# Bucket projections in four column parts, weight conversions in three stages, the queries' low part on GpSimd

## The chip, the cores and the metric

The kernel runs on one core of one Trainium2 chip. The metric is the device time of that core in microseconds (us). An engine name stands for its queue too: PE is TensorE, DVE is VectorE, ACT is ScalarE, POOL is GpSimd and SP is SyncE, which here only issues DMAs. Each engine works its own list of instructions strictly in order, and an instruction whose operands aren't there holds up everything behind it on its engine.

## The reference, cut to what matters

Two batches, 8 heads, 768 rows, head dimension 64, six hash bits. Attention is masked by bucket: a query sees a key only if the signs of their six projections agree. Two feed-forward blocks follow.

```python
q_bits = (np.einsum('bhsd,dk->bhsk', q, proj) > 0)      # six bits each
k_bits = (np.einsum('bhsd,dk->bhsk', k, proj) > 0)
mask = q_bucket[:, :, :, None] == k_bucket[:, :, None, :]
scores = np.where(mask, scale * q @ k.T, -1e9)
attn = softmax(scores); out = attn @ v
x = moe(out)      # relu(x w_in) = u, v; LayerNorm(v); w_spatial v + b; u * v; w_out
y = x + relu(LayerNorm(x) * g @ w_ch1) @ w_ch2
```

## The kernel before, in words

Everything is in single precision made of two parts: a value is rounded to a high part in TensorE's fp32r format, and what is left over is the low part; products are made as high*high + high*low + low*high. The weights arrive as 64-bit floats and are turned into single precision on the chip.

**Attention** is 96 tiles of 128 queries: batch, head, group of two tiles (order, line 249). A pair of heads (b, r), heads 2r and 2r+1, is loaded together, transposed, as 128 rows (two heads of 64) by 768 columns. Of a pair, pair_load (206) fetches k and q into the slot where later the low part stands; mismatch (236) multiplies the raw data by a small matrix of signs, `side`, and turns the result by one comparison into rows of 0, 1 or 2**60 (tile `m`); pair_split (218) makes the high parts on POOL (line 228, first pair: ACT), the keys' low part on POOL in two halves (86) and the queries' low part on DVE (234). The low part overwrites the raw data, so it waits for mismatch's matmuls. passes_of (258) lets SP copy high, low and mismatch rows into the operand tiles ks (a head's keys) and qs (a group's queries), lines 269, 270 and 275. A tile then goes through scores (L299, PE), masked_max (L310, DVE), exps (L323, ACT), transposes (L337 PE, L340 ACT, L342 DVE) and weighted (L351 PE, L356 ACT, L358 DVE).

The steps of a pair come a fixed number of tiles ahead of its first tile: AT = (-10, -7, -6, -4, 0) for load, mismatch, split, first and second head's ks. qs of a group is made QA + 1 = 4 tiles ahead.

**Conversions.** Twelve pieces of the weights w_out, w_in's v half and w_in's u half are converted during the attention (conversions, line 484; names out, v, u). Each is a DMA by ACT's queue (stage), one ACT and five DVE instructions (words_f64, lines 102 to 107), a sum on POOL (111), then a high part on ACT (80) and a low part on POOL (86). CONV_AT gives the tile at which a piece's words are issued, CONV_D the four steps' distances from it, (-1, 0, 3, 3). There is one buffer (CB0 = 1) for a piece.

**Feed-forward.** From tile M0 = 60 on, moe1 of batch 0 is interleaved (pv, pg, py on PE); after the attention come moe1 of batch 1 and the last block with w1 and w2 (pc and acc), whose pieces are converted as they come (load_f64).

The order of each engine's list is not that of the source: a scheduler runs through a model of the engines and lists instructions as they become ready there; issue_after keeps some of them behind the last max or exp.

Of the kernel before, what the change touches and what calls it, by code (L numbers as in the profile page):

```python
# [8 lines left out]
F32 = mybir.dt.float32  # L9
# [8 lines left out]
P = 128  # L18
# [11 lines left out]
def attn_moe_kernel(ctx: ExitStack, tc: tile.TileContext, qT, kT, v, proj, w_in, w_spT, b_sp, w_out, g_ln, w1, w2, out):  # L30
# [18 lines left out]
    CONV_D = (-1, 0, 3, 3)  # L49
# [46 lines left out]
    def words_f64(st, nm):  # L96

        a, n = st.shape[1], st.shape[2]
# [19 lines left out]
    def load_f64(dst_hi, dst_lo, src, nm):  # L118

        split_f64(dst_hi, dst_lo, join_f64(*words_f64(stage_f64(src, nm), nm)))  # L120
# [14 lines left out]
    K_FROM, Q_FROM = 38, 0  # L135
    M_AT = {"k": (D, NB), "q": (D + 32, 32 + NB)}
    sides = const.tile([P, K_FROM + P], F32, name="sides")
    nc.gpsimd.memset(sides, 0.0)
    for own, at in zip((slice(0, D), slice(D, P)), M_AT["q"]):
        for i, sign in enumerate((1.0, -1.0, 1.0)):  # L140
            nc.gpsimd.tensor_scalar(
                sides[own, at + i * NB : at + (i + 1) * NB], pj[own], sign, 0.0, op0=ALU.mult, op1=ALU.add
            )
    side = {"k": sides[:, K_FROM : K_FROM + P], "q": sides[:, Q_FROM : Q_FROM + P]}
# [3 lines left out]
    for t, fills in (  # L148
        (above, ((0, P, 0.0), (0, NM, -TINY), (32, NB + NM, -TINY), (32, NM, 0.0), (D, NB, -TINY))),
        (above, ((D + 32, NM, -TINY), (D + 32, NB, 0.0))),  # L150
        (worth, ((0, P, 1.0), (32, NB + NM, MASKED), (D + 32, NM, MASKED))),
    ):
        for at, n, value in fills:
            nc.gpsimd.memset(t[at : at + n], value)
# [63 lines left out]
    def pair_split(b, r, first=False):  # L218

        for nm in "kq":  # L220
# [8 lines left out]
            if nm == "k" and not first:  # L229
# [6 lines left out]
    def mismatch(b, r):  # L236


        m = ap.tile([P, S], F32R, tag="m", name=f"m_{b}_{r}", bufs=2)
# [215 lines left out]
    def converted(src, dst, nm, after=None):  # L455
# [6 lines left out]
        def words():  # L462
            d["tc"] = words_f64(d["st"], nm)
# [411 lines left out]
```

## Time and profile before

| | us |
|---|---|
| median of 3 runs | 736.6 (736.15 to 738.83) |
| the profiled execution's own time | 737.13 |
| its span, first to last instruction | 734.9 |
| PE, DVE, ACT, POOL busy | 686.0, 438.7, 303.6, 190.9 |
| mean granted clock of TensorE | 0.98 of 2.4 GHz |

The table gives one core's engines over the whole span. A share of the span is a mean over stages: the attention lasts until about 347 us, where the last weighted sum (po) is seen, and the feed-forward alone fills what follows. PE is busy 93% of the span, so the shares say that PE's work, not its waiting, is most of the time; which of it can go is read from the stages.

### The profile page before, as it was taken

How to read it: one execution, taken by the hardware profiler on the slowest of the kernel's cores; microseconds unless marked ns; L12 is line 12 of the kernel's file. 1: busy time of each engine (PE TensorE's matmuls, PEld its weight loads, DVE VectorE, ACT ScalarE, POOL GpSimd, SP SyncE). 2: the span in 40 equal slices, each digit the busy share in tenths (PEclk: the TensorE clock that was granted, in tenths of full speed). 3: DMA queues.
4: the chain of work that ended last, by engine and by line, in shares of the span. 5: the costliest groups of instructions: out<-in, count | busy, mean ns of one | idle time of the engine just before them, and what ended most of it. 6: DMA issues, size and time to landing. Idle time of an engine off the chain costs nothing.

```text
span 734.9 us, 9990 instructions
## 1 busy us (share of the span) xinstructions
PE 686.0 (93%) x3580; PEld 533.1 (73%) x3580; DVE 438.7 (60%) x849; ACT 303.6 (41%) x583; POOL 190.9 (26%) x182
## 2 busy tenths in 40 slices
PE   6999999898999999998889999799988999999997
PEld 5767667675767777776678887587766788888885
DVE  3698987897665645444798459676899712112112
ACT  2676766685556545344364222453323201100100
POOL 2234143334352222110144243244544400000000
PEclk8899999999999999999999999899999999999999
DMA  6765866674554554212625153523232101001001
GB/s 168 187 159 155 248 163 179 207 195 122 156 175 98 178 179 102 80 38 72 220 62 197 44 165 122 199 90 114 89 112 86 58 1 57 1 0 58 1 0 58
DMA packets 51922, 84.37 MB, mean 115 GB/s; under 512 B 6970, under 2 KB 36206, under 8 KB 50850
## 3 DMA queue, kind: packets, MB, share of 16 engines
q1 hardware_dynamic: 38834, 54.37, 25.8%
q10 hardware_dynamic: 13040, 29.36, 12.3%
q8 instruction: 29, 0.48, 0.3%
q14 instruction: 19, 0.16, 0.1%
HBM read 51.12 MB, written 12.58 MB: 87 GB/s over the span
## 4 chain that ended last, share of the span: by engine, by line
PE 60%; DVE 15%; DMA 11%; ACT 4%; issue 4%; POOL 3%; SPq 1%; DVEq 0%; ACTq 0%; POOLq 0%
PE acc L747 12%; PE pc L437 11%; PE sc L299 7%; DMA f_w<-in_w 7%; PE pv L437 7%; PE pt L337 6%; PE pg L607 6%; PE po L351 6%; PE py L437 3%; POOL f64c_w L111 2%; DVE f_w L105 2%; DVE x L310 2%; DMA qs<-q 2%; DMA f_v<-in_w_in 1%; DVE f64c_w L107 1%
## 5 line engine op out<-in xcount | busy, mean ns | idle before, releaser
L747 PE MATMUL acc<-w2t,ch 128*128 128x512 f32 x576 | 145.3, 398 | 6.6 <-DVE ch L738 5.2
L437 PE MATMUL pc<-xh,w1t 128*128 128x512 f32 x576 | 146.9, 400 | 3.9 <-DVE xh L731 2.7
L747 PEld LDWEIGHTS acc<-w2t,ch 128*128 128x128 f32 x576 | 107.5, 189 | 34.5 <-DVE ch L738 8.1
L437 PEld LDWEIGHTS pc<-xh,w1t 128*128 128x128 f32 x576 | 110.0, 192 | 30.0 <-ACT f64c_w L102 2.9
L310 DVE TENSOR_SCALAR_CACHE_REDUCE x<-sc 128x768 f32<-128x768 f32 x96 | 89.5, 950 | 23.1 <-PE sc L299 22.9
L323 ACT ACTIVATE x<-x,nb 128x768 f32<-128x768 f32 x96 | 89.3, 931 | 32.7 <-DVE x L310 32.6
L738 DVE SCALAR_TENSOR_TENSOR ch<-pc,ch 128x512 fp32r<-128x512 f32 x48 | 33.0, 688 | 112.6 <-ACT ch L737 112.6
L299 PE MATMUL sc<-ks,qs 128*128 128x512 f32 (+3 forms) x384 | 86.3, 363 | 9.2 <-PE po L351 3.1
L337 PE MATMUL pt<-ident,x 128*128 128x128 f32 x576 | 79.8, 278 | 9.8 <-ACT x L323 9.3
L337 PEld LDWEIGHTS pt<-ident,x 128*128 128x128 f32 x576 | 67.6, 143 | 26.7 <-ACT x L323 17.6
L737 ACT ACTIVATE ch<-pc 128x512 fp32r<-128x512 f32 x48 | 28.5, 593 | 131.5 <-PE pc L437 131.5
L299 PEld LDWEIGHTS sc<-ks,qs 128*128 128x128 f32 (+1 forms) x384 | 59.8, 199 | 21.6 <-PE po L351 6.2
L351 PE MATMUL po<-e,vv 128*64 128x256 f32 x576 | 74.1, 393 | 0.4 <-DVE m L246 0.4
L111 POOL TENSOR_TENSOR f64c_w<-f_w,f64c_w 128x512 f32<-128x512 f32 x32 | 43.7, 1368 | 93.9 <-DVE f64c_w L107 77.9
L340 ACT ACTIVATE e<-pt 128x384 f32<-128x384 f32 x96 | 46.5, 488 | 45.4 <-PE pt L337 44.5
L342 DVE COPY e<-pt 128x384 f32<-128x384 f32 x96 | 52.7, 549 | 20.7 <-PE pt L337 20.2
L351 PEld LDWEIGHTS po<-e,vv 128*64 128x64 f32 x576 | 37.5, 138 | 24.4 <-issue 7.3
L102 ACT ACTIVATE f64c_w<-f_w 128x512 f32<-128x512 f32 x32 | 21.4, 669 | 63.0 <-DMA f_w<-in_w 59.6
L607 PE MATMUL pg<-vn,w_sp 128*128 128x512 f32 x180 | 44.1, 397 | 0.0
L437 PE MATMUL pv<-w_u,act_x 128*128 128x512 f32 x144 | 37.8, 398 | 4.7 <-DMA w_u<-ws_u 2.8
L607 PEld LDWEIGHTS pg<-vn,w_sp 128*128 128x128 f32 x180 | 33.3, 188 | 7.6
L437 PE MATMUL py<-w_out,act_g 128*128 128x512 f32 x144 | 35.8, 396 | 2.1 <-ACT act_g L426 2.1
(131 smaller groups left out, 813.3 us busy)
## 6 DMA issues: line engine op xcount, KB each, us to landing
f_w<-in_w ACTq DMA_DIRECT2D x32, 512.0 KB
ks<-k SPq DMA_DIRECT2D x48, 192.0 KB
qs<-q SPq DMA_DIRECT2D x144, 64.0 KB
wst_sp<-in_w_spT SPq DMA_DIRECT2D x12, 384.0 KB
w_out<-ws_out SPq DMA_DIRECT2D x2, 2048.0 KB
vv<-in_v SPq DMA_DIRECT2D x16, 192.0 KB
ot<-y_dram SPq DMA_DIRECT2D x12, 256.0 KB
out<-ot SPq DMA_DIRECT2D x12, 256.0 KB
```

Of the source, the lines that this page charges most:

```text
L111: nc.gpsimd.tensor_tensor(cf, tf, cf, op=ALU.add)
L299: nc.tensor.matmul(sc[:, csl], qs[:rows, i, qsl], ks[:rows, i, csl], start=(i == 0), stop=(i == 1))
L310: last["max"] = nc.vector.tensor_scalar(x, t["sc"], MASKED, FMAX, op0=ALU.min, op1=ALU.min, accum_out=nb,).ins
L323: last["exp"] = nc.scalar.activation(t["x"], t["x"], AF.Exp, bias=t["nb"], scale=-1.0, accum_out=z_sum[b][:, n, h : h + 1]).ins
L337: nc.tensor.transpose(pt[:, i, :], t["x"][:, kt * P : (kt + 1) * P], ident)
L340: nc.scalar.activation(e, pt, AF.Copy)
L342: nc.vector.tensor_copy(e, pt)
L351: nc.tensor.matmul(po[a : a + D, :GW], heads[b, h]["vv"][:, kt], gr["e"][:, kt], start=(kt < 2), stop=(kt >= NKT - 2))
L437: mm = nc.tensor.matmul(ps, lh(i), rh(j), start=(n == 0), stop=(n == tot - 1)).ins
L607: nc.tensor.matmul(pg, w[i][:, k], vn[:, j, k, :], start=(n == 0), stop=(n == len(order3) - 1))
L738: last["lo"] = nc.vector.scalar_tensor_tensor(ch[:, 1], pc, 0.0, ch[:, 0].bitcast(F32), op0=ALU.max, op1=ALU.subtract).ins
L747: last["mm"] = nc.tensor.matmul(accs[c][t], ch[:, i, t * P : (t + 1) * P], w2t[f][:, j, 0, :], start=(start and n == 0), stop=(stop and n ...
```

## The change: what it does

**1. Projections.** `side` is now 32 columns wide for keys and for queries (`sides` has 38 columns instead of 166), and the eight matmuls of a pair write four parts of 32 partitions each of one 128x512 PSUM tile: keys of one half, keys of the last third, queries of one half, queries of the last third, 256 columns at a time. Before, four matmuls with 128 weight columns over 384 data columns filled two 128x384 tiles, keys and queries accumulated. One comparison over 128x512 takes the place of two over 128x384. The mismatch rows of columns 512 to 767 lie in other partitions than those of columns 0 to 511, so ks takes two copies for them.

**2. qs.** The high part goes to both its places by one DMA with a repeated source: three DMAs a group instead of four; ks has five instead of four.

**3. Conversions.** words_f64 became a generator with three stages: ACT's instruction and the first DVE one; two DVE ones; the last two. CONV_D is (-1, 0, 1, 2, 4, 4): the stages are one tile apart, sum and finish one tile later than before.

**4. The queries' low part** of all pairs but the first is made by POOL: one more instruction scales the raw queries in place (128x768), and two subtract the high part (128x384 each). DVE's instruction of line 234 remains for the first pair alone.

```diff
-    CONV_D = (-1, 0, 3, 3)
+    CONV_D = (-1, 0, 1, 2, 4, 4)
...
         nc.vector.tensor_scalar(cf, cf, F64_MIN, F64_MAX, op0=ALU.max, op1=ALU.min)
+        yield
         nc.vector.tensor_scalar(c, c, 3, 0x3FFFFFFF, op0=ALU.logical_shift_left, op1=ALU.bitwise_and)
         nc.vector.scalar_tensor_tensor(hi, hi, 0xC0000000, c, op0=ALU.bitwise_and, op1=ALU.bitwise_or)
+        yield
         nc.vector.tensor_scalar(c, hi, 0xFF800000, None, op0=ALU.bitwise_and)
         nc.vector.scalar_tensor_tensor(cf, lo, 2.0**-52, cf, op0=ALU.mult, op1=ALU.mult)
-        return hi.bitcast(F32), cf
+        yield hi.bitcast(F32), cf
...
-    sides = const.tile([P, K_FROM + P], F32, name="sides")
+    sides = const.tile([P, NB + QUAD], F32, name="sides")
...
-            if nm == "k" and not first:
+            if not first:
+                if nm == "q":
+
+                    nc.gpsimd.tensor_scalar(raw, raw, scale, 0.0, op0=ALU.mult, op1=ALU.add)
                 for c in range(2):
                     csl = slice(c * KC, (c + 1) * KC)
                     split_lo(lo[:, csl], raw[:, csl], hi[:, csl])
...
-        for c in range(2):
-            csl = slice(c * KC, (c + 1) * KC)
-            pm = ps_b.tile([P, 512], F32, tag="b", name=f"pm_{b}_{r}_{c}")
-            for i, nm in enumerate("kq"):
+        m = ap.tile([P, 2 * GW], F32R, tag="m", name=f"m_{b}_{r}", bufs=2)
+        pm = ps_b.tile([P, 2 * GW], F32, tag="b", name=f"pm_{b}_{r}")
+
+        for half in range(2):
+            for n, (nm, g) in enumerate((("k", half), ("k", 2), ("q", half), ("q", 2))):
                 raw = pairs[b, r][nm, "raw"]
-                nc.tensor.matmul(pm[:, :KC], side[nm], raw[:, csl], start=(i == 0), stop=(i == 1))
-            nc.vector.tensor_scalar(m[:, csl], pm[:, :KC], above, worth, op0=ALU.is_gt, op1=ALU.mult)
+                out_n = pm[n * QUAD : (n + 1) * QUAD, half * GW : (half + 1) * GW]
+                nc.tensor.matmul(out_n, side[nm], raw[:, g * GW : (g + 1) * GW], start=True, stop=True)
+        nc.vector.tensor_scalar(m, pm, above, worth, op0=ALU.is_gt, op1=ALU.mult)
...
+            nc.sync.dma_start(out=t[0:D].bitcast(F32), in_=two[own, 0:1, sl].to_broadcast([D, 2, n]))
+            nc.sync.dma_start(out=t[D:P, 0].bitcast(F32), in_=two[own, 1, sl])
...
-        return stage, words, join, finish
+        return stage, words, words, words, join, finish
```

On PE, at the mismatch of pair (0, 1), the four matmuls of the kernel before stand between the weighted sum of a group (po) and the next transposes (pt); pm is the PSUM tile.

```order
L351 MATMUL po_0_1_350<-e_0_1_245,vv_0_175 64x256 x6
L245 MATMUL pm_1_0_361<-k_0_1_270,sides 128x384
L245 MATMUL pm_1_0_361<-q_0_1_272,sides 128x384
L245 MATMUL pm_1_1_365<-k_0_1_270,sides 128x384
L245 MATMUL pm_1_1_365<-q_0_1_272,sides 128x384
L337 MATMUL pt_1_0_0_0_377<-ident,x_1_0_0_346 128x128 x3
```

In the changed kernel the same place holds eight, in the order keys, keys, queries, queries, twice.

```order
L366 MATMUL po_0_1_356<-e_0_1_253,vv_0_184 64x256 x6
L252 MATMUL pm_1_367<-k_0_1_277,sides 32x256 x2
L252 MATMUL pm_1_367<-q_0_1_279,sides 32x256 x2
L252 MATMUL pm_1_367<-k_0_1_277,sides 32x256 x2
L252 MATMUL pm_1_367<-q_0_1_279,sides 32x256 x2
L352 MATMUL pt_1_0_0_0_381<-ident,x_1_0_0_352 128x128 x3
```

The place is the same; only the matmuls themselves and their shapes differ.

On DVE, at the same pair, a whole conversion (f_out and f64c_out), both comparisons (m), the queries' low part (q) and a sum (xT) stand in one run ahead of the max of the next tile (x_1_1_0) in the kernel before.

```order
L103 TENSOR_SCALAR f64c_out_369<-f64c_out_369 128x512
L104 TENSOR_SCALAR f64c_out_369<-f64c_out_369 128x512
L105 SCALAR_TENSOR_TENSOR f_out_330<-f_out_330,f64c_out_369 128x512
L246 TENSOR_SCALAR m_1_360<-pm_1_0_361,above,worth 128x384
L358 TENSOR_TENSOR xT_177<-po_0_1_350,ol_0_1_357 64x256
L106 TENSOR_SCALAR f64c_out_369<-f_out_330 128x512
L246 TENSOR_SCALAR m_1_360<-pm_1_1_365,above,worth 128x384
L234 SCALAR_TENSOR_TENSOR q_0_1_272<-q_0_1_272 128x768
L107 SCALAR_TENSOR_TENSOR f64c_out_369<-f_out_330,f64c_out_369 128x512
L310 TENSOR_SCALAR x_1_1_0_420,nb_1_1_0_421<-sc_1_1_0_387 128x768
```

In the changed kernel the max of that tile stands after four instructions of this work, and the conversion's last two come behind it, each after a max.

```order
L104 TENSOR_SCALAR f64c_out_377<-f64c_out_377 128x512
L106 TENSOR_SCALAR f64c_out_377<-f64c_out_377 128x512
L253 TENSOR_SCALAR m_1_366<-pm_1_367,above,worth 128x512
L107 SCALAR_TENSOR_TENSOR f_out_336<-f_out_336,f64c_out_377 128x512
L373 TENSOR_TENSOR xT_186<-po_0_1_356,ol_0_1_363 64x256
L357 COPY e_1_0_380<-pt_1_0_0_1_386 128x3x128
L325 TENSOR_SCALAR x_1_1_0_427,nb_1_1_0_428<-sc_1_1_0_391 128x768
L109 TENSOR_SCALAR f64c_out_377<-f_out_336 128x512
L325 TENSOR_SCALAR x_1_1_1_459,nb_1_1_1_460<-sc_1_1_0_391 128x768
L357 COPY e_1_0_380<-pt_1_0_1_1_418 128x3x128
L110 SCALAR_TENSOR_TENSOR f64c_out_377<-f_out_336,f64c_out_377 128x512
```

What moved is the max, from behind nine instructions to behind six.

On POOL, at pair (1, 1), where the first block of batch 0 also begins (act_x are its low parts, f64c_u and w_u a conversion's), the kernel before has the keys' low part (k_1_1) as its only low part.

```order
L86 TENSOR_TENSOR act_x_0_2192<-xT_177,act_x_0_2192 128x512
L86 TENSOR_TENSOR act_x_1_2195<-xT_177,act_x_1_2195 128x512
L228 TENSOR_SCALAR q_1_2_2296<-q_1_2_2296 128x768
L86 TENSOR_TENSOR act_x_2_2245<-xT_177,act_x_2_2245 128x512
L86 TENSOR_TENSOR k_1_1_1851<-k_1_1_1851 128x384 x2
L111 TENSOR_TENSOR f64c_u_1816<-f_u_1786,f64c_u_1816 128x512
```

In the changed kernel the queries' scaling follows the keys' low part, and four other instructions stand between it and the queries' low part (q_1_1).

```order
L86 TENSOR_TENSOR act_x_0_2195<-xT_186,act_x_0_2195 128x512
L86 TENSOR_TENSOR k_1_1_1854<-k_1_1_1854 128x384 x2
L235 TENSOR_SCALAR q_1_1_1856<-q_1_1_1856 128x768
L86 TENSOR_TENSOR act_x_1_2198<-xT_186,act_x_1_2198 128x512
L86 TENSOR_TENSOR act_x_2_2253<-xT_186,act_x_2_2253 128x512
L114 TENSOR_TENSOR f64c_u_1669<-f_u_1637,f64c_u_1669 128x512
L231 TENSOR_SCALAR q_1_2_2303<-q_1_2_2303 128x768
L86 TENSOR_TENSOR q_1_1_1856<-q_1_1_1856 128x384 x2
```

The keys' low part moved ahead of two of the act_x instructions; the queries' low part, before on DVE, comes last of the eight.

## Rows read from the trace of the kernel before

**Rows 1.** The page, part 1: busy us (share of the span) xinstructions.

```profile
PE 686.0 (93%) x3580; PEld 533.1 (73%) x3580; DVE 438.7 (60%) x849; ACT 303.6 (41%) x583; POOL 190.9 (26%) x182
```

**Rows 2.** Stretches: length, busy us of each engine, PEclk, DMA share, GB/s.

```profile
50.00:100.00 50.00, 47.15 (x323) 34.63 (x322) 44.95 (x96) 35.19 (x74) 18.65 (x18) 1.00 0.66 194
100.00:150.00 50.00, 45.29 (x306) 33.19 (x306) 41.90 (x93) 32.45 (x68) 15.01 (x15) 0.97 0.65 182
150.00:200.00 50.00, 46.25 (x299) 34.03 (x299) 39.06 (x85) 33.17 (x70) 20.20 (x18) 1.00 0.56 144
200.00:250.00 50.00, 48.76 (x290) 37.40 (x290) 28.38 (x70) 27.44 (x57) 16.40 (x16) 1.00 0.56 170
```

**Rows 3.** Chain that ended last, from 0 to 280 us: start us, us, what.

```profile
8.77 4.25 DMA qs<-q
...
37.47 1.21 DVE q L234
...
63.18 1.45 PE po L351 x12
64.62 2.78 PE pm L245 x8
...
158.26 3.38 DMA qs<-q
```

**Rows 4.** Timeline of PE, 33 to 42.5 us: start us, us, engine line op.

```profile
35.05 0.81 PE L245 MATMUL pm<-q,sides 128*128 128x384 f32 x2
35.70 0.49 PE L337 MATMUL pt<-ident,x 128*128 128x128 f32 x3
...
41.27 0.87 PE L337 MATMUL pt<-ident,x 128*128 128x128 f32 x6 [1.23 <-ACT x L323]
```

**Rows 5.** Instructions of lines 246, 234, 228, 86, 269: duration ns min/median/max.

```profile
L246 DVE TENSOR_SCALAR m<-pm,above,worth x16: 656/670/677, 8.9 to 265.2; 128x384 fp32r<-128x384 f32 x16
L234 DVE SCALAR_TENSOR_TENSOR q<-q x7: 948/1157/2093, 37.4 to 265.8; 128x768 fp32r<-128x768 f32 x7
L228 POOL TENSOR_SCALAR q<-q x7: 832/838/1086, 26.2 to 211.3; 128x768 fp32r<-128x768 f32 x7
L86 POOL TENSOR_TENSOR k<-k x14: 993/1004/1715, 34.1 to 264.6; 128x384 fp32r<-128x384 f32 x14
L269 SPq DMA_DIRECT2D qs<-q x96: 461/575/2039, 7.5 to 304.0; - x96
```

**Rows 6.** Timeline, pair (0, 2): PE, then POOL and SP.

```profile
64.55 0.91 PE L245 MATMUL pm<-k,sides 128*128 128x384 f32 x2
78.10 1.65 PE L299 MATMUL sc<-ks,qs 128*128 128x512 f32 x8 [0.94 <-PE po L351]
...
69.27 1.72 POOL L86 TENSOR_TENSOR k<-k 128x384 fp32r<-128x384 f32 x1
...
70.15 0.52 SPq L269 DMA_DIRECT2D qs<-q  x1
```

**Rows 7.** Timeline, pair (0, 3): POOL, then SP and PE.

```profile
102.51 0.83 POOL L228 TENSOR_SCALAR q<-q 128x768 fp32r<-128x768 f32 x1 [2.67 <-DMA ks<-k]
...
101.67 2.17 SPq L269 DMA_DIRECT2D qs<-q  x3
...
109.27 1.65 PE L299 MATMUL sc<-ks,qs 128*128 128x512 f32 x8 [0.21 <-PE po L351]
```

**Rows 8.** Timeline, pair (1, 1) and after: POOL, then PE.

```profile
161.41 2.56 POOL L86 TENSOR_TENSOR act_x<-xT,act_x 128x512 fp32r<-128x512 f32 x2 [2.29 <-ACT act_x L80]
170.96 1.30 POOL L111 TENSOR_TENSOR f64c_u<-f_u,f64c_u 128x512 f32<-128x512 f32 x1
...
165.15 0.81 PE L245 MATMUL pm<-q,sides 128*128 128x384 f32 x2
176.54 1.67 PE L299 MATMUL sc<-ks,qs 128*128 128x512 f32 x8 [0.33 <-PE po L351]
197.36 2.58 PE L437 MATMUL pv<-w_u,act_x 128*128 128x512 f32 x10
```

More of the change, by code (lines that the diff above doesn't have):

```diff
@@ L118, in load_f64 @@
     def load_f64(dst_hi, dst_lo, src, nm):
-        split_f64(dst_hi, dst_lo, join_f64(*words_f64(stage_f64(src, nm), nm)))
+        split_f64(dst_hi, dst_lo, join_f64(*list(words_f64(stage_f64(src, nm), nm))[-1]))
     const = ctx.enter_context(tc.tile_pool(name="const", bufs=1))
@@ L132, in attn_moe_kernel @@
     nc.sync.dma_start(out=pj, in_=proj.rearrange("(o d) n -> o d n", o=1).to_broadcast([2, D, NB]))
-    K_FROM, Q_FROM = 38, 0
-    M_AT = {"k": (D, NB), "q": (D + 32, 32 + NB)}
-    sides = const.tile([P, K_FROM + P], F32, name="sides")
+    HROW = 3 * NB
+    QUAD = 32
+    sides = const.tile([P, NB + QUAD], F32, name="sides")
     nc.gpsimd.memset(sides, 0.0)
-    for own, at in zip((slice(0, D), slice(D, P)), M_AT["q"]):
+    for a, own in enumerate((slice(0, D), slice(D, P))):
         for i, sign in enumerate((1.0, -1.0, 1.0)):
[L141 to L144, printed above, removed]
+            at = a * HROW + i * NB
+            nc.gpsimd.tensor_scalar(sides[own, at : at + NB], pj[own], sign, 0.0, op0=ALU.mult, op1=ALU.add)
+    side = {"k": sides[:, NB : NB + QUAD], "q": sides[:, 0:QUAD]}
     above = const.tile([P, 1], F32, name="above")
     worth = const.tile([P, 1], F32, name="worth")
[L148 to L154, printed above, removed]
+    nc.gpsimd.memset(above, 0.0)
+    nc.gpsimd.memset(worth, 1.0)
+    for at in range(0, P, QUAD):
+        keys = ((4 * NB, -TINY), (3 * NB, 0.0), (NB, -TINY))
+        queries = ((5 * NB, -TINY), (4 * NB, 0.0), (2 * NB, -TINY), (NB, 0.0))
+        for n, value in keys if at < 2 * QUAD else queries:
+            nc.gpsimd.memset(above[at : at + n], value)
+    nc.gpsimd.memset(worth[2 * QUAD : P], MASKED)
     b_sb = const.tile([P, NQT], F32, name="b_sb")
@@ L264, in passes_of @@
         pr = pairs[b, h // 2]
-        at = M_AT[nm][h % 2]
         two = pr[nm].bitcast(F32)
         own = slice(h % 2 * D, (h % 2 + 1) * D)
-        for a in range(2):
-            nc.sync.dma_start(out=t[a * D : (a + 1) * D, 0].bitcast(F32), in_=two[own, a, sl])
-        nc.sync.dma_start(out=t[0:D, 1].bitcast(F32), in_=two[own, 1 - LOW[nm], sl])
-        rows = pr["m"][at : at + NM, sl].bitcast(F32)
-        if first:
-            nc.vector.tensor_copy(t[D:MR, 1], rows)
-        else:
-            nc.sync.dma_start(out=t[D:MR, 1].bitcast(F32), in_=rows)
+        if nm == "k":
+            for a in range(2):
+                nc.sync.dma_start(out=t[a * D : (a + 1) * D, 0].bitcast(F32), in_=two[own, a, sl])
+            nc.sync.dma_start(out=t[0:D, 1].bitcast(F32), in_=two[own, 1, sl])
+        else:
+            nc.sync.dma_start(out=t[0:D].bitcast(F32), in_=two[own, 0:1, sl].to_broadcast([D, 2, n]))
+            nc.sync.dma_start(out=t[D:P, 0].bitcast(F32), in_=two[own, 1, sl])
+        for lo, hi in ((0, 2 * GW), (2 * GW, S)):
+            lo, hi = max(sl.start, lo), min(sl.stop, hi)
+            if lo < hi:
+                at = (2 * "kq".index(nm) + lo // (2 * GW)) * QUAD + h % 2 * HROW
+                rows = pr["m"][at : at + NM, lo % (2 * GW) : lo % (2 * GW) + hi - lo].bitcast(F32)
+                to = t[D:MR, 1, lo - sl.start : hi - sl.start]
+                if first:
+                    nc.vector.tensor_copy(to, rows)
+                else:
+                    nc.sync.dma_start(out=to.bitcast(F32), in_=rows)
         return t
@@ L462, in words @@
         def words():
-            d["tc"] = words_f64(d["st"], nm)
+            if "w" not in d:
+                d["w"] = words_f64(d["st"], nm)
+            d["tc"] = next(d["w"])
         def join():
```

1 line of the change is left out of this document (removed).

## The prediction

> **What bounds the kernel now.** The page's first part comes first: PE is busy 686 of 734.9 us [rows 1]. The view by stretches of 50 us then tells where the rest is. The reader should subtract PE's busy time from 50 in each row: between 50 and 250 us, the attention, 2.9, 4.7, 3.7 and 1.2 us are left, 12.5 in all, and DVE is the busiest after PE there, 45 of 50 us in the first of these rows [rows 2]. So the attention is bound by PE, with short waits where DVE has too much at once. The chain of waits shows both kinds: the bucket projections of one pair stand in it as 2.78 us of PE, and elsewhere the same stage stands in it as DVE's queries [rows 3]. Such a DVE run ends in a PE wait of 1.23 us for an exp, which had waited for the max behind the run [rows 4]. What follows the attention is fed by PE and by weight conversions that start when their turn comes; I find no wait there that an earlier end of the attention wouldn't move forward with the rest.
>
> **The projections.** Before, one pair issues four matmuls, each as two records of 384 columns. Two records take 0.65 us from start to start (35.05 to 35.70 [rows 4]), so one takes 0.325 and eight 2.6. Afterwards there are sixteen records of 256 columns, 0.325 x 256/384 = 0.217 us each. Whether they run beside each other decides. The trace has a form that shows it: po writes two halves of 64 partitions, and its twelve records of 256 columns take 1.45 us up to the next matmul [rows 3], where one after the other they would take 2.6 and two abreast 1.3; the rest, 0.15, I take for entering and leaving the column form. Four abreast, sixteen records take 16/4 x 0.217 + 0.15 = 1.0 us, two abreast 1.9, singly 3.6. A gain of 1.6, a gain of 0.7, or a loss of 1.0 us a pair. I take four abreast: 64-column parts reach their full two, and 32-column parts are the same form one step smaller. Seven of the eight pairs lie within the attention: 7 x 1.6 = 11.2 us. The first pair's block is hidden: the first scores wait for a qs copy that runs from 8.77 for 4.25 us [rows 3].
>
> The Trainium skill (TensorE: Matmul & The Clock Gate, Part 3, packing) gives 2.38 times for three column tiles of 32, which is less than the full three that po's 1.45 us would suggest. By it, as an estimate, four parts run about 3.2 abreast and the block takes 1.2 us, so the gain would be 9.8 instead of 11.2 us.
>
> **DVE.** A pair loses two comparisons of 0.67 and the low part of 1.16 (median) [rows 5], 2.5 us, and gets one comparison of 512 columns, between 0.67 and twice that; by length 0.9. That is 1.6 us less a pair, 11 us over seven pairs, out of 154 us busy between 50 and 250 us [rows 2]. None of it adds to the 11.2 directly, since PE is the bound; it shortens the waits. The conversions keep all their instructions, but in pieces a tile apart, so that the next max stands behind six instructions instead of nine (the order of DVE in the section on the change). Of the 12.5 us of waits this can give back between nothing and all. I take 5: less than half, because the waits at 176.54 and 109.27 us are PE waiting on itself or on copies [rows 7, 8].
>
> **SP.** A group's qs takes one DMA fewer, a head's ks one more: 48 - 16 = 32 issues of some 0.58 us fewer [rows 5]. SP isn't in the chain for long, so only the first one counts, ahead of the scores that wait for qs at the start: 0.6 us.
>
> **POOL.** Each of seven pairs adds a scaling of 0.84 and two subtractions of 1.0 [rows 5], 2.84 us in place of DVE's 1.16; 20 us for an engine that is busy 26% [rows 1]. The work itself is hidden beside PE. What isn't is its place: the queries' low part now ends after the keys' low part instead of beside it, and then SP must copy it before the pair's first scores. The cover, from the issue of that copy to the first scores, is 78.10 - 70.15 = 8.0 us at pair (0, 2) [rows 6] and 109.27 - 101.67 = 7.6 at pair (0, 3) [rows 7]; a qs copy has taken up to 3.4 us [rows 3], so some 4.5 us are left. At (0, 2) the keys' low part ends at 70.99; 2.84 more, less the 1.3 of a conversion's sum that no longer stands in between, is 72.5, or 2.4 later than before: covered. At (0, 3) the next pair's scaling, which started at 102.51 when its load had landed [rows 7], moves ahead of the keys' low part: 103.3 + 2.0 + 2.84 = 108.2, or 6.5 later: 2 us too late. At (1, 1) the order puts two act_x, a sum and another scaling in between. Act_x takes 1.28 and the sum 1.30 [rows 8]; counted from the end of the first act_x, 162.7, or from that of the projections, 165.8 [rows 8], the list holds 2.0 + 0.84 + 2.6 + 1.3 + 0.84 + 2.0 = 9.6 us and ends between 172.3 and 175.4. The scores start at 176.54 [rows 8], a copy of up to 3.4 us lies between: 0 to 2.3 us late. The waits queue up on SP too: behind a waiting copy stand the copies of the following groups, which have two tiles' time.
>
> Where the conversions end a tile later, the last piece of w_u is the one that is needed soon: pv reads w_u from 197.36 on [rows 8], and a tile is some 2.6 us (twelve from 78.10 to 109.27 [rows 6, 7]). The scheduler lists pv later accordingly, with scores and transposes ahead. For all new waits I take 5 us: two pairs of 2 and 1 for the rest. The bounds are 0, if the cover holds everywhere, and 20, below.
>
> **The sum**, against the profiled execution's own 737.1 us: 737.1 - 11.2 - 5 - 0.6 + 5 = 725.3. This execution lies 0.5 above the median of the runs shown, so the forecast is 724.8 us.
>
> **Rivals.**
>
> Two abreast only. If the fp32 halves of a matmul bind each part to its neighbour, the gain is 0.7 a pair: 724.8 + 7 x 0.9 = 731.1 us. For it: po's form has shown two and nothing more. Against it: its records come in pairs, one for each of its two parts, so both parts there are always filled.
>
> DVE's waits go altogether and the copies are never late: 12.5 instead of 5, and 0 instead of 5 lost, 712.3 us. For it: 11 us less on DVE and shorter runs. Against it: some waits are not DVE's.
>
> The queries' low part becomes the bound, and the kernel slower. In place: POOL's list ahead of the first scores of the pairs (0, 1) to (1, 1), whose cover is some 4.5 us. From the point where the low part ends 4.5 us later than before, PE stands still for the rest; with the delays of (0, 3) everywhere, 6.5 - 4.5 = 2, and as each pair arrives some 2 us sooner than before, 4 us at five pairs: 20 instead of 5, so 739.8 us. For it: POOL waits for the next pair's load in front of this work. Against it: (0, 2) is covered by the list as it stands. The Trainium skill (GPSIMD Engine Reference, 3.1) says the same in general, that VectorE is to be used for elementwise work, with a two-input addition 1.96 times as long on GpSimd; here it is 2.0 for the two halves against 1.16, so the trace agrees on the price, and only the cover decides.
>
> The parts run singly, so that the change doesn't do what it is written for: 1.0 a pair lost instead of 1.6 won, 724.8 + 7 x 2.6 = 743.0 us. Against it: po.
>
> **How the numbers follow.** Forecast 0.54 (its own range 718 to 731), two abreast 0.16, waits gone 0.10, low part late 0.14, singly 0.06. Leaving out the last and the ends of the others, the range is 713 to 740. Half a per cent, 3.7 us, is about what a measurement can tell from no change. Below 732.9 lie nearly all of the forecast, three quarters of two abreast and the third case: 0.76. Above 740.3 lie the last case and half of the one before it, with some of the unforeseen: 0.14. Between them 0.10.
>
> **What would show it.** Right: pm's block takes about 1.0 us from its first matmul to the next, with four starts close together; DVE loses some 11 us and POOL gains 20; PE's idle time from 50 to 250 us falls below 12.5. Wrong: pm at 1.9 us or above; PE waiting for a DMA of qs ahead of a pair's first scores, POOL's line 86 behind it; ACT or DVE waiting for a conversion's buffer. If the attention ends 11 us earlier and the total doesn't, a conversion of w1 or w2 after it has taken the gain back.

## The result and the profile after

The changed kernel takes 742.8 us (median of 20 runs, 736.91 to 749.08) against 737.02 (735.24 to 741.04): ratio 1.0072, 95% interval 1.0054 to 1.0090. It is slower by more than the half per cent that counts here; the forecast was 724.8, and 742.8 lies above its range. One of the 20 runs, 749.08, was in a slower state and is not in the ratio.

The first part of its page answers to [rows 1]: PE and DVE lost work, POOL gained some, and the span grew by 7.3 us.

```profile
span 742.2 us, 10044 instructions
## 1 busy us (share of the span) xinstructions
PE 681.1 (92%) x3644; PEld 529.0 (71%) x3644; DVE 432.0 (58%) x835; ACT 302.5 (41%) x583; POOL 213.4 (29%) x210
```

The view by stretches of 50 us, beside [rows 2]: PE's busy time, then the other engines', then the granted clock as a share of 2.4 GHz.

```profile
50.00:100.00 50.00, 45.63 (x352) 33.19 (x350) 41.54 (x88) 33.59 (x71) 19.52 (x19) 1.00 0.67 179
100.00:150.00 50.00, 41.73 (x314) 30.72 (x310) 41.34 (x90) 33.24 (x70) 20.78 (x21) 1.00 0.63 157
150.00:200.00 50.00, 40.21 (x248) 29.12 (x248) 32.14 (x70) 27.63 (x59) 20.65 (x19) 0.86 0.55 160
200.00:250.00 50.00, 48.43 (x299) 36.21 (x297) 30.47 (x71) 28.16 (x58) 21.22 (x20) 1.00 0.54 160
```

Subtract from 50 again: 4.4, 8.3, 9.8 and 1.6 us are left, 24.0 where there were 12.5. PE waits twice as long although it has less to do.

The block itself became what was forecast. PE's timeline at pair (0, 1): from the first matmul at 32.98 to the next work at 33.98 it takes 1.0 us, and starts come in fours.

```profile
31.53 1.51 PE L366 MATMUL po<-e,vv 128*64 128x256 f32 x12
32.98 0.41 PE L252 MATMUL pm<-k,sides 128*32 128x256 f32 x2
32.99 0.41 PE L252 MATMUL pm<-q,sides 128*32 128x256 f32 x2
33.22 0.39 PE L252 MATMUL pm<-k,sides 128*32 128x256 f32 x2
33.23 0.39 PE L252 MATMUL pm<-q,sides 128*32 128x256 f32 x2
...
33.98 0.88 PE L352 MATMUL pt<-ident,x 128*128 128x128 f32 x6
```

Where the time went is told by two marks, read from the traces: the start of the attention's last score matmul, and the last matmul of all. The first moved from 331.5 to 335.0, and what lies between them grew from 397.7 to 401.1 us. So half of the 7 us was lost in the attention and half behind it. In the attention the kernel was ahead until pair (1, 1): pair (1, 0) starts its scores at 140.5 instead of 144.5, the head before (1, 1) at 154.6 instead of 159.1, but (1, 1) itself at 183.0 instead of 176.5. The timeline of ACT, PE, POOL and SP there, beside [rows 8]:

```profile
159.76 0.66 ACT L103 ACTIVATE f64c_u<-f_u 128x512 f32<-128x512 f32 x1 [2.78 <-DMA f_u<-in_w_in]
161.39 1.54 PE L352 MATMUL pt<-ident,x 128*128 128x128 f32 x6 [3.75 <-ACT e L355]
162.87 2.83 PE L366 MATMUL po<-e,vv 128*64 128x256 f32 x12
167.40 2.15 POOL L86 TENSOR_TENSOR k<-k 128x384 fp32r<-128x384 f32 x2 [1.32 <-PE pm L252]
169.53 1.27 POOL L235 TENSOR_SCALAR q<-q 128x768 f32<-128x768 f32 x1
170.76 2.51 POOL L86 TENSOR_TENSOR act_x<-xT,act_x 128x512 fp32r<-128x512 f32 x2
173.24 1.30 POOL L114 TENSOR_TENSOR f64c_u<-f_u,f64c_u 128x512 f32<-128x512 f32 x1
174.51 0.83 POOL L231 TENSOR_SCALAR q<-q 128x768 fp32r<-128x768 f32 x1
175.32 1.96 POOL L86 TENSOR_TENSOR q<-q 128x384 fp32r<-128x384 f32 x2
178.01 0.57 SPq L280 DMA_DIRECT2D qs<-q  x1
183.02 2.08 PE L314 MATMUL sc<-ks,qs 128*128 128x512 f32 x8 [2.69 <-DMA qs<-q]
```

PE waits twice. First it waits 3.75 us for a copy on ACT, which stands in ACT's list behind the wait of 2.78 us for the load of f_u, a conversion's input; behind that wait po's twelve records take 2.83 us instead of 1.51, at a granted clock of 0.50 from 161.4 to 164.0, the lower of the clock's two levels, 1.2 GHz. Then it waits 2.69 us for qs: POOL works without a pause from 167.40 on, the queries' low part ends at 177.28, its copy is issued at 178.01 and the scores start at 183.02. Between 18 and 330 us ACT's waits for the loads of f_out, f_v and f_u are 20.9 us, where they were 10.3.

Behind the attention one wait is clearly longer, at a place on which the change has no line. VectorE's gt, which the next transposes need, stands behind words and statistics. Before:

```profile
452.67 0.74 DVE L609 SCALAR_TENSOR_TENSOR gt<-pg,b_sb,xT 128x512 f32<-128x512 f32 x1
453.46 0.66 PE L424 MATMUL ptr_g<-ident,gt 128*128 128x128 f32 x4 [1.78 <-DVE gt L609]
```

After, with the clock at its lower level behind the wait (0.50 granted from 458.9 to 461.0, and 1.09 us for the same transposes):

```profile
458.01 0.74 DVE L626 SCALAR_TENSOR_TENSOR gt<-pg,b_sb,xT 128x512 f32<-128x512 f32 x1
458.89 1.09 PE L439 MATMUL ptr_g<-ident,gt 128*128 128x128 f32 x4 [5.21 <-DVE gt L626]
```

This wait alone isn't the account of the 3.4 us. Over the whole rest PE's idle time grows by 1.4 us only, from 21.5 to 22.9, and its busy time by 2.0, from 376.7 to 378.6 at a granted clock of 0.97 instead of 0.98. In e2 below the same wait is 4.37 us, and the rest is no longer than before.

### The profile page after: what moved, and what is told of

Read it like the earlier page. It is cut to its first block, busy times and chain, and to the rows that moved or that the text cites. A ratio compares the mean times of both kernels' runs of the same rounds, so it can differ in the third digit from the quotient of the medians.

```text
span 742.2 us, 10044 instructions
## 1 busy us (share of the span) xinstructions
PE 681.1 (92%) x3644; PEld 529.0 (71%) x3644; DVE 432.0 (58%) x835; ACT 302.5 (41%) x583; POOL 213.4 (29%) x210
## 4 chain that ended last, share of the span: by engine, by line
PE 56%; DMA 15%; DVE 13%; POOL 5%; issue 4%; ACT 4%; SPq 2%; DVEq 0%; ACTq 0%; POOLq 0%
PE acc L764 12%; PE pc L452 10%; PE pv L452 8%; PE pg L624 6%; PE sc L314 6%; PE po L366 5%; DMA f_w<-in_w 5%; PE pt L352 4%; PE py L452 3%; DMA f_v<-in_w_in 3%; DMA f_u<-in_w_in 2%; DVE f_w L107 2%; POOL f64c_w L114 2%; DMA qs<-q 1%; DMA f_out<-in_w_out 1%
## 5 line engine op out<-in xcount | busy, mean ns | idle before, releaser
L352 PEld LDWEIGHTS pt<-ident,x 128*128 128x128 f32 x576 | 68.7, 144 | 28.4 <-ACT x L338 10.8
L357 DVE COPY e<-pt 128x384 f32<-128x384 f32 x96 | 52.8, 550 | 20.9 <-PE pt L352 20.7
L624 PE MATMUL pg<-vn,w_sp 128*128 128x512 f32 x180 | 46.5, 411 | 0.0
```

The lines of the kernel that those rows point to most:

```text
L352: nc.tensor.transpose(pt[:, i, :], t["x"][:, kt * P : (kt + 1) * P], ident)
L357: nc.vector.tensor_copy(e, pt)
L624: nc.tensor.matmul(pg, w[i][:, k], vn[:, j, k, :], start=(n == 0), stop=(n == len(order3) - 1))
```

## The experiments

Each ratio is to the kernel before, run beside it, with its 95% interval. "Scores" is the start of the attention's last score matmul and "rest" what follows up to the last matmul, both from the one profiled execution. Executions of one kernel differ by 3 to 12 us in all, so a difference of a few us between two marks is not sure by itself.

| run | ratio | scores, us | rest, us |
|---|---|---|---|
| before | 1 | 331.5 | 397.7 |
| the change | 1.0072 (1.0054 to 1.0090) | 335.0 | 401.1 |
| e1 column parts alone | 1.0024 (0.9998 to 1.0051) | 330.3 | 400.0 |
| e2 stages alone | 1.0030 (1.0008 to 1.0052) | 330.0 | 397.3 |
| e3 GpSimd's queries alone | 1.0072 (1.0048 to 1.0097) | 336.8 | 398.9 |
| e4 change, join sooner | 1.0079 (1.0046 to 1.0112) | 333.9 | 398.1 |
| e5 parts, matmuls x3 | 1.0223 (1.0197 to 1.0249) | 348.5 | 398.8 |
| e6 parts, no queries' low | 0.9894 (0.9865 to 0.9924) | 322.5 | 397.5 |
| e7 before, no queries' low | 0.9923 (0.9897 to 0.9949) | 326.0 | 396.2 |
| e8 parts, earlier loads | 1.0014 (0.9992 to 1.0037) | 331.1 | 396.4 |
| e9 before, half the matmuls | 0.9946 (0.9925 to 0.9966) | 325.1 | 398.7 |
| e10 parts, no keys' low | 0.9904 (0.9877 to 0.9932) | 323.0 | 398.3 |
| e11 before, no keys' low | 1.0045 (1.0021 to 1.0070) | 331.4 | 402.1 |
| e12 parts, pieces moved | 1.0006 (0.9981 to 1.0031) | 328.0 | 396.1 |
| e13 parts, raw keys apart | 0.9909 (0.9878 to 0.9940) | 324.5 | 399.7 |
| e14 e3 but for (1, 1) | 1.0011 (0.9990 to 1.0031) | 335.0 | 396.6 |
| e15 parts, GpSimd's queries, raws apart | 1.0024 (1.0005 to 1.0042) | 330.4 | 398.9 |
| e16 change, raws apart | 0.9984 (0.9957 to 1.0010) | 327.0 | 404.8 |
| e17 before, raw keys apart | 1.0108 (1.0074 to 1.0142) | 330.6 | 409.9 |
| e18 parts, raws apart | 1.0037 (1.0014 to 1.0059) | 324.6 | 406.2 |

### The three edits, one at a time

e1 undoes two of them in the changed kernel (VectorE's branch returns for the queries):

```diff
-    CONV_D = (-1, 0, 1, 2, 4, 4)
+    CONV_D = (-1, 0, 0, 0, 3, 3)
...
-            if not first:
-                if nm == "q":
-                    nc.gpsimd.tensor_scalar(raw, raw, scale, 0.0, op0=ALU.mult, op1=ALU.add)
+            if nm == "k" and not first:
```

> The changed kernel with two of its three parts undone: only the column parts (and the copies that go with them) stay; the conversions issue all words at once and join three tiles later, and VectorE makes the queries' low part. If the staged conversions (theory A) or GpSimd's low part (theory B) took the gain back, this kernel shows what the parts alone give: seven blocks 1.6 us shorter, 11 us, so about 726 us against 737, with the first scores of pair (1, 1) near 166 us instead of 183. If the parts themselves or their copies cost (theory C, one more DMA per keys' tile, one comparison that comes later than two), it stands at 737 or above.

e2 puts the generator and CONV_D = (-1, 0, 1, 2, 4, 4) into the kernel before.

> The kernel before with the staged conversions alone. Theory A: a piece's join stands at its fourth tile instead of its third, the pieces are four or five tiles apart and there is one buffer, so the next load starts when its words are already due and ACT, in order, holds the exps and copies behind it for some 2 us a piece: 742 to 750 us, with ACT's idle time ahead of its first step (abs) waiting for the f_v and f_u loads at 15 us or more, against 9 before. Theories B and C: 735 to 738.

e3 puts the branch of e1's diff, taken the other way, into the kernel before.

> The kernel before with GpSimd making the queries' low part and nothing else. Theory B: the scores of pairs (0, 1) to (1, 1) wait for the copy of qs, 4 to 11 us in all: 741 to 748 us, PE waiting at the first scores of pair (1, 1) for a DMA of qs. Theory A: VectorE has 1.16 us less a pair and the copies are covered but for (1, 1): 735 to 739.

e4 changes the changed kernel's CONV_D to (-1, 0, 1, 2, 3, 3).

> The changed kernel with one number changed: the three stages of words stay a tile apart, but the join and the finish come in the third tile instead of the fourth, one tile sooner, so the buffer comes free a tile sooner. Theory A: the next load starts some 2.6 us earlier, ACT's wait for it shrinks from about 18 us for f_v and f_u to under 10, and the time falls from 742.8 to 728 to 735. Theory B: still 741 to 744, and pair (1, 1) still waits for its qs.

e1: 737.51 us. The parts give nothing, theory C's number. e2: 737.73, some 2 us lost, which its one profiled execution shows in neither stretch; ACT waits 11.7 us for f_v and f_u, not the 15 of theory A. Theory A falls for the stages alone. e4: 741.58, but it doesn't test A: ACT's waits for f_v and f_u go from 18.2 to 16.8 us only, not under 10, and the load of f_u ahead of (1, 1) is issued at 154.14, as in the change (154.19). e3: 741.11, as slow as the whole change: theory B's number, and scores 5.3 us late. The three losses one by one, 0.24, 0.30 and 0.72%, are together more than the change's 0.72, so the edits don't simply add. Two questions are left: where e1's gain is, and what of e3 costs.

### Does PE's time count?

e5, in e1's kernel:

```diff
-                nc.tensor.matmul(out_n, side[nm], raw[:, g * GW : (g + 1) * GW], start=True, stop=True)
+                for _ in range(3):
+                    nc.tensor.matmul(out_n, side[nm], raw[:, g * GW : (g + 1) * GW], start=True, stop=True)
```

> The column parts alone (the first run), with every one of the projections' matmuls issued three times into the same place: 2 x 1.04 us more of PE a pair, 14.6 us over the seven pairs inside the attention, and nothing else. Theory D: the stretch around the projections isn't bound by PE but by the round of scores, VectorE's max, exp and transposes, with VectorE's comparison, queries and conversion words ahead of the max; PE has free time there of about the size of the gain that was lost, so the time rises by less than half of 14.6: 738 to 743. If PE is the bound (the prediction's step): 749 to 753.

e9, in the kernel before:

```diff
-            for i, nm in enumerate("kq"):
-                raw = pairs[b, r][nm, "raw"]
-                nc.tensor.matmul(pm[:, :KC], side[nm], raw[:, csl], start=(i == 0), stop=(i == 1))
+            nm = "kq"[c]
+            raw = pairs[b, r][nm, "raw"]
+            nc.tensor.matmul(pm[:, :KC], side[nm], raw[:, csl], start=True, stop=True)
```

> The kernel before with two of a pair's four projection matmuls left out (keys for the first half of the columns only, queries for the second; the other half of the mismatch rows is not computed): 1.3 us instead of 2.6 us of PE a pair, 9.1 us over seven pairs, and the order and copies of the kernel before. If PE's time in that block counts (tripling it in the column parts cost all of 14.6 us): 727 to 730, and it is something else in the column parts that took their gain back. If the block stands beside a longer path in the kernel before: 734 to 738.

e5: 751.73 us; by the ratios 1.0223 - 1.0024, 14.6 us more than e1. That is the number of the second reading, but by chance, since the edit added more than 14.6. Three matmuls in a row into the same part don't run beside each other as those into four parts do, and the block takes 4.64 us up to the next work, not 3.1:

```profile
34.21 1.30 PE L250 MATMUL pm<-k,sides 128*32 128x256 f32 x8
...
37.65 1.27 PE L250 MATMUL pm<-q,sides 128*32 128x256 f32 x8
38.85 0.87 PE L350 MATMUL pt<-ident,x 128*128 128x128 f32 x6
```

So 3.64 us a pair were added, 25.5 over seven pairs, and the total shows 14.6 of them, 57%; the last scores come 18.2 us later. e9: 732.64, 0.54% or 4.0 us for the 9.1 us taken away, 44%; its expectation took over the "all of 14.6" and is wrong there too. Neither reading holds as it was put: in both directions about half of what the block gains or loses reaches the total, and for the other half PE stands beside another path. The 10.9 us of e5 that don't show are about the free time that theory D gave PE.

### What VectorE's and POOL's low parts hold

e6 and e7 replace, in e1's kernel and in the one before, the `else:` of VectorE's low part by `elif first:`.

> The column parts alone, and VectorE's low part of the queries left out for seven pairs (the queries' low part is then not computed; everything that reads it stays). Takes 9.4 us from VectorE, none from PE. Theory D: the maxes come up to 1.3 us sooner at each pair and the time falls by 4 to 9 us, to 729 to 733. If PE or the copies are the bound: 736 to 738.

> The control to the run above: the kernel before with the same low part of the queries left out (not computed). Theory D: here PE has the full 2.6 us block beside which VectorE works, so less is gained than with the parts: 733 to 737. If VectorE sets the end alike in both, both gain the same.

e8, in e1's kernel:

```diff
-    CB0 = 1
+    CB0 = 2
-    CONV_D = (-1, 0, 0, 0, 3, 3)
+    CONV_D = (-4, 0, 0, 0, 3, 3)
```

> The column parts alone, with two buffers for a conversion's input in the attention and its load issued four tiles ahead of its words instead of one. In the trace of the parts alone, PE waits 4.3 us in four places for a copy on ACT that stands behind ACT's wait for the load of f_v or f_u. If that wait is a part of the lost gain: 732 to 735, and ACT waits for f_v and f_u under 3 us in all. If VectorE's run alone sets the end: 737 to 738.

e10 and e11 drop POOL's `split_lo(lo[:, csl], raw[:, csl], hi[:, csl])` in e1's kernel and in the one before.

> The column parts alone, with POOL's low part of the keys left out for seven pairs (not computed). Theory F: in the parts' trace all of POOL's work for a pair starts when the short block ends and meets VectorE's queries and words (queries 1.55 us instead of 0.95, a word 1.30 instead of 0.7), and VectorE's instructions in the first 345 us are stretched by 8.3 us against 3.3 before; without the keys' low part the stretch falls under 4 us and the time to 727 to 732. If POOL's work isn't what took the gain: 736 to 738.

> The control to the run above: the kernel before with the same low part of the keys left out (not computed). Theory F: there POOL's halves follow the two halves of a longer block and collide less, so less is gained: 733 to 736. If the keys' low part sets the end in both alike, both gain the same.

e12, in e1's kernel:

```diff
-    CONV_AT = (5, 9, 14, 19, 24, 29, 34, 39, 44, 49, 53, 57)
+    CONV_AT = (7, 11, 15, 19, 23, 27, 31, 35, 39, 43, 47, 51)
```

> The column parts alone, with the conversions' tiles moved: (7, 11, 15, 19, ... 51) instead of (5, 9, 14, 19, ... 57), every four tiles, so that no piece's words stand in the tiles of a pair's comparison and low part (5, 6, 17, 18, 29, 30, ...). If VectorE's run of comparison, queries and words ahead of the max is what costs at a pair: 729 to 734. If the pieces, now closer together, or another order of the lists decide: 737 or above.

e6: 727.9, e7: 730.16 us, both below what was expected. VectorE's 9.4 us are worth some 9.6 us with the parts, and its 8.6 before are worth 5.7; so VectorE's run is a good part of the path beside PE. e8: 736.05, e12: 736.7; neither is told from e1. In e8 ACT's waits for f_v and f_u, 10.5 us in e1, are gone, while those for POOL's sums grow from 10.4 to 13.9; so neither ACT's waits for loads nor the tiles of the pieces by themselves took the gain. e10: 729.57, and the parts have their gain: scores 8.4 us sooner than e11's. VectorE's stretch (over all its instructions up to 345 us, the time of each less the median of those of its form beside which POOL stands still, or less the shortest where there is none) is 3.2 us there, as in the kernel before, where e1 has 8.4. e11's own time, 739.48, was not expected: less work and 0.45% slower. Its attention is that of the kernel before (331.4), and its rest holds the same wait for gt, 6.06 us; the scheduler's lists had changed behind the attention too.

### The repair, and its control

e13, in e1's kernel, gives the raw keys a tile of their own, so that POOL's low part needn't wait for the block. All of the work stays.

```diff
                 raw = pr[nm][:, LOW[nm]].bitcast(F32)
+                if nm == "k":
+                    raw = ap.tile([P, S], F32, tag="rawk", name=f"kraw_{b}_{r}", bufs=1)
```

> The column parts alone, with the raw keys of a pair in a tile of their own (3 KB more a partition), so that POOL's low part of the keys no longer overwrites what the projections read and can run as soon as the load has landed, ahead of the block. All work stays. Theory F (what took the gain is POOL's work behind the block, beside VectorE's): as without the keys' low part, 728 to 732. If only leaving the work out helps, or the order of the lists decides: 736 to 740.

e17 is the same edit in the kernel before.

> The control: the kernel before with the raw keys of a pair in a tile of their own and no other change. Theory F: POOL's halves already follow the two halves of the long block there, so nothing is gained: 735 to 739, and the gain of e13 belongs to the column parts once they are freed. If the repair alone gives e13's gain: 729 to 732.

e18 takes such a tile for keys and queries in e1's kernel.

> The column parts alone with raw keys and raw queries in tiles of their own; VectorE still makes the queries' low part, but needn't wait for the projections. If the run of comparison, queries and words ahead of the max holds the rest of the gain: 725 to 728. If the early place costs as much as it gives: 729 to 733, as e13.

e13: 730.4 us, faster than both kernels, 0.9% below the one before. e17: 744.74, which no theory said; but ahead of the last scores it is where the kernel before is (330.6), and what it loses is lost behind (409.9 instead of 397.7 in the profiled execution): PE waits 5.5 us for w_u's reload and 5.5 for ACT, where it waits 2.8 and 0.6 in the kernel before, and over the rest its busy time is 6.8 us longer at a granted clock of 0.96 instead of 0.98. e18: 739.31, above both its readings: the attention is as short as e13's (324.6), and again the loss is behind it (406.2). So the tile of their own takes 5.8 us off the parts' attention and 0.9 off that of the kernel before; what the total shows depends on the lists behind.

The traces of e1 and e13 at the same place, pair (0, 3), show a mechanism at work, since VectorE's list is the same there: m, q, the word L107, e, max, max. In e1:

```profile
99.27 1.97 POOL L86 TENSOR_TENSOR k<-k 128x384 fp32r<-128x384 f32 x2 [6.28 <-PE pm L249]
99.79 0.79 DVE L250 TENSOR_SCALAR m<-pm,above,worth 128x512 fp32r<-128x512 f32 x1
100.50 1.55 DVE L237 SCALAR_TENSOR_TENSOR q<-q 128x768 fp32r<-128x768 f32 x1
101.21 1.54 POOL L231 TENSOR_SCALAR q<-q 128x768 fp32r<-128x768 f32 x1
101.98 1.30 DVE L107 SCALAR_TENSOR_TENSOR f_v<-f_v,f64c_v 128x512 uint32<-128x512 uint32 x1
104.55 0.94 DVE L322 TENSOR_SCALAR_CACHE_REDUCE x<-sc 128x768 f32<-128x768 f32 x1
105.60 1.66 PE L311 MATMUL sc<-ks,qs 128*128 128x512 f32 x8 [2.03 <-issue]
```

In e13, where POOL has nothing to do from 90 to 101.84:

```profile
94.14 0.80 DVE L252 TENSOR_SCALAR m<-pm,above,worth 128x512 fp32r<-128x512 f32 x1
94.85 0.94 DVE L239 SCALAR_TENSOR_TENSOR q<-q 128x768 fp32r<-128x768 f32 x1
95.72 0.68 DVE L107 SCALAR_TENSOR_TENSOR f_v<-f_v,f64c_v 128x512 uint32<-128x512 uint32 x1
97.66 0.95 DVE L324 TENSOR_SCALAR_CACHE_REDUCE x<-sc 128x768 f32<-128x768 f32 x1
98.72 1.66 PE L313 MATMUL sc<-ks,qs 128*128 128x512 f32 x8 [0.79 <-PE po L365]
```

The queries take 1.55 instead of 0.94 us beside POOL and the word 1.30 instead of 0.68, together 1.23; PE's wait is 2.03 instead of 0.79, 1.24 more. "issue" is PE waiting for the second of two maxes, which frees the scores' PSUM tile: PE starts just after it, in both. The waits of e1 by what ended them, from 18 to 330 us (total, times, longest):

```profile
PE sc L311 <- issue: 9.9, 5, 2.2
PE pm L249 <- ACT e L352: 4.3, 4, 1.5
PE pt L349 <- ACT x L335: 3.3, 3, 1.8
```

and of the kernel before, where neither of the first two is found but for one wait of 2.0 at the start:

```profile
PE pt L337 <- ACT x L323: 9.3, 10, 2.1
PE sc L299 <- PE po L351: 3.1, 6, 0.9
PE sc L299 <- issue: 2.0, 1, 2.0
```

The Trainium skill (SBUF — State Buffer, "Who interferes with whom") says that a VectorE instruction with two inputs in SBUF contends with a GpSimd instruction that reads SBUF, and that one with at most one such input doesn't, outside its two-port modes. The trace agrees: the queries and the word L107 have two such inputs and stretch, and the maxes, which read PSUM, take 0.92 to 0.96 us in both kernels, beside POOL or not.

The stretch is only a part of e13's 5.8 us: it falls from 8.4 to 5.1. POOL's list changes as well: ACT's waits for POOL's sums fall from 10.4 to 1.4 us, and PE's waits for ACT ahead of the block (second row of e1's list) from 4.3 to 0.2. No run parts the two. Nor is the shorter block alone what brings POOL and VectorE together. The eight matmuls read keys up to the sixth of them, the last third twice, so both of POOL's halves come free near the block's end; before, the first half was free after the first matmul. At (0, 3) POOL starts 1.1 us into the block before (97.61 from 96.55), but in e5 3.4 us into it (106.92 from 103.50), although that block is the longer one. Another order of the eight, keys first, was not tried.

### The queries' low part on GpSimd

e14, in e3's kernel:

```diff
-            if not first:
+            if not first and (nm == "k" or (b, r) != (1, 1)):
```

> The kernel before with GpSimd making the queries' low part for all pairs but (1, 1), where VectorE makes it as before. If the cost of 4.7 us comes from POOL's list at (1, 1), where three act_x, a conversion's sum and its low part stand in the same tiles: 733 to 737. If it is paid a little at every pair: 740 to 741.

e15 is e1's kernel with POOL's queries, e16 the whole change; both with raw keys and queries in tiles of their own, the scaled queries written to the low part's slot.

```diff
-                raw = pr[nm][:, LOW[nm]].bitcast(F32)
+                raw = ap.tile([P, S], F32, tag="raw" + nm, name=f"{nm}raw_{b}_{r}", bufs=1)
...
-                    nc.gpsimd.tensor_scalar(raw, raw, scale, 0.0, op0=ALU.mult, op1=ALU.add)
+                    nc.gpsimd.tensor_scalar(lo.bitcast(F32), raw, scale, 0.0, op0=ALU.mult, op1=ALU.add)
+                    raw = lo.bitcast(F32)
```

> The column parts and GpSimd's low part of the queries, conversions not staged, with raw keys and raw queries in tiles of their own, so that both low parts can be made ahead of the block. If the cost of GpSimd's low part is its place behind the projections and not its 20 us of work: 725 to 730, as where the low part was left out (727.9 with the parts). If POOL's time as such or its collisions with VectorE cost: 735 to 743.

> The whole changed kernel, staged conversions too, with raw keys and raw queries in tiles of their own. Against the run before it, this one shows what the stages give once the low parts are out of the way: with the place of the low parts as the cause, 724 to 731 instead of 742.8; otherwise 739 or above.

e14: 738.15 us, between the two readings. Its trace bears theory B out only in part: from the first scores of (1, 0) to those of (1, 1) it takes 37.6 us, where e3 takes 41.1 and the kernel before 32.0, so (1, 1) still starts late, at 180.6. e3 shows what they share. The scheduler has put the high part of the next pair's queries (L228) ahead of three act_x; it waits for the copies that still read that tile, and with it wait act_x, the keys' low part and a conversion's sum (L111). ACT's w_u waits for the sum and holds the exps; the next load of f_u is issued behind w_u, and ACT waits for that too:

```profile
168.52 0.83 POOL L228 TENSOR_SCALAR q<-q 128x768 fp32r<-128x768 f32 x1 [6.20 <-DMA qs<-q]
169.32 3.75 POOL L86 TENSOR_TENSOR act_x<-xT,act_x 128x512 fp32r<-128x512 f32 x3
174.01 1.29 POOL L111 TENSOR_TENSOR f64c_u<-f_u,f64c_u 128x512 f32<-128x512 f32 x1
175.33 0.63 ACT L80 ACTIVATE w_u<-f64c_u 128x512 fp32r<-128x512 f32 x1 [3.43 <-POOL f64c_u L111]
176.93 0.88 PE L340 MATMUL pt<-ident,x 128*128 128x128 f32 x6 [2.48 <-ACT x L326]
180.47 0.66 ACT L102 ACTIVATE f64c_u<-f_u 128x512 f32<-128x512 f32 x1 [2.66 <-DMA f_u<-in_w_in]
182.47 1.54 PE L340 MATMUL pt<-ident,x 128*128 128x128 f32 x6 [3.22 <-ACT x L326]
```

In e14 the sum's time is 173.33 and ACT waits 5.18 us for it; in the kernel before the sum runs at 170.96 [rows 8]. So in e3 PE doesn't wait for the low part's own copy at (1, 1); what is late is POOL's list. Leaving the low part's own items out of it there (e14) gives back 3.5 of the 9.1 us that e3 loses between those two marks.

e15: 738.55. Freed from the block, (1, 1) starts at 172.9, yet the scores end no sooner than in e1: the same parts without GpSimd's queries and with the same tiles, e18, are 5.8 us ahead (324.6) in the attention, while the totals of the two are alike. POOL's work now meets other work: VectorE's stretch, counted as above, is 10.8 us, the most of all these kernels. From 113.31 on the profile names POOL's queries as what holds ACT's next abs (1.46 us), behind which stand a copy and PE's po (2.17 us). But the load that abs needs was issued at 110.77, and in the kernel before such a load is waited for until 4.3 to 4.5 us after its issue, so that which of the two held it is not shown.

```profile
113.31 1.94 POOL L86 TENSOR_TENSOR q<-q 128x384 fp32r<-128x384 f32 x2
115.33 0.66 ACT L103 ACTIVATE f64c_v<-f_v 128x512 f32<-128x512 f32 x1 [1.46 <-POOL q L86]
116.56 1.51 PE L367 MATMUL po<-e,vv 128*64 128x256 f32 x12 [2.17 <-ACT e L356]
```

e16: 736.43 us, between its two readings; the attention is 8 us shorter than the changed kernel's, and 3.7 are lost again behind it.

## Why the prediction was wrong, point by point

**The block: right.** 1.0 us, four abreast, as taken from po's form. "Two abreast" and "singly" are out, and so is the lower estimate of 1.2 us.

**The step that failed first: "Seven of the eight pairs lie within the attention: 7 x 1.6 = 11.2 us".** The size per pair was right, but not that all of it counts, which the prediction took from PE being the bound. e1 has PE's work down by 10.4 us over the first 735 (675.67 against 686.05) and is no faster. The runs showed two things in place of that step. First, about half of what the block gains or loses reaches the total: 14.6 of 25.5 us in e5, 4.0 of 9.1 in e9, and in e13, where the parts do gain, 6.7 of 11.2. PE's 93% busy does not say that each of its microseconds counts. Second, in e1 that half was taken back. The prediction knew that the keys' low part waits for the block, and did not ask what it meets then: before, at pair (0, 3), POOL's halves ran at 97.61 and 98.84, done ahead of VectorE's queries at 100.69; in e1 both start at the block's end and run beside them. Freed from the block, in e13, the attention is 5.8 us shorter than e1's. How much of that is the stretch and how much POOL's list stays open.

**"Of the 12.5 us of waits ... I take 5": wrong in sign.** They grew to 24.0. DVE lost 6.7 us of the 11 expected. That its run matters was right (e6, e7: 5.7 to 9.6 us if the queries vanish); but the work didn't vanish, and POOL's work stretches what VectorE keeps.

**"The work itself is hidden beside PE": wrong.** e3 alone costs 0.72% or 5.3 us after VectorE's relief is counted, nearly all of it between the first scores of (1, 0) and (1, 1), 41.1 us instead of 32.0. What the prediction did price there came out near it: POOL's list at (1, 1) took 9.9 us for 9.6, the copy 5.0 for 3.4, and PE waited 2.69 us for it, where 0 to 2.3 were forecast; at (0, 2) and (0, 3) nothing came late, their first scores start 2 us sooner than before. But (1, 1) starts 6.5 us late. Left out was what hangs on the conversions in these lists: in the change ACT's wait for f_u and PE's 3.75 us behind it, with the clock at its lower level; in e3 the sum and with it ACT's list. Both signs that were named are there, PE waiting for a copy of qs with POOL's line 86 behind it, and ACT waiting for a conversion's load. The rule of the Trainium skill (GPSIMD Engine Reference, 3.1), elementwise work on VectorE, would have been the better guide: the prediction weighed it by the instruction's own price, and by the cover alone.

**The stages:** cost some 2 us alone, by e2. What they do in the whole change is open: ACT's waits for the loads of f_out, f_v and f_u are 20.9 us there, 13.2 with the stages alone, 13.5 with the parts alone and 15.0 with GpSimd's queries alone, and no run has the change as it is without the stages. With raws apart they bring the last scores 3.4 us sooner (e16 against e15). **SP's issue** at the start: the first scores start at 13.5 against 13.3, nothing gained.

**The rival that came nearest** in its mechanism is the third, the queries' low part as the bound, 739.8 us, with POOL's list as its place. It lacked that the parts give nothing beside it. By the number alone the last, 743.0, is nearest, by luck: the parts don't run singly. Of the rest, 3.4 us stand behind the attention: that something there could take time back was named as a sign, but not priced. No edit touches that code, yet the engines' lists differ there, and the wait for gt is 1.4 to 6.1 us long in these kernels. What makes the scheduler's lists come out one way or the other was not tried, so this part of the loss is shown and its cause left open.

## What to carry to other kernels

A busy share of 93% doesn't make every microsecond of that engine count: lengthen and shorten the block first, measure the block itself each time, and see how much reaches the total. When such a block gets shorter or reads its operands in another order, look at what was waiting for it: engines that used to follow one after the other now start together, and the saving can be paid out where two of them share a path. Count instructions moved to GpSimd twice, once in its own list with all that stands behind them, and once in the VectorE instructions beside which they will run. And where a scheduler makes the lists, compare stage by stage (here the attention and the rest apart) before a total of half a per cent is put down to an edit.

## What the runs showed of the hardware that had not been expected

- VectorE instructions with SBUF operands stretch beside POOL: queries 0.94 to 1.55 us, a word 0.68 to 1.30; POOL's high part of the queries 0.84 to 1.54 in the same place. Max (0.92 to 0.97) and copies from PSUM (0.49 to 0.57) don't.
- Sixteen fp32 records of 256 columns in four parts of 32 partitions take 1.0 us, where one after the other they would take 3.5. With each matmul issued three times in a row into its part the forty-eight take 4.64, not three times 1.0 (e5).
- PE waits of 3.75 and 5.21 us were each followed by a granted clock at its lower level (0.50), po 2.83 us instead of 1.51, so that a wait there cost more than its length.
